# Three places in a RetNet and MLP kernel: where the down products fall back, in which banks a run begins, and when its last sums are formed

## The chip, the cores and the metric

The kernel runs on one core of a Trainium2 chip. A core has TensorE (PE in the profile), which multiplies matrices into PSUM; VectorE (DVE), ScalarE (ACT) and GpSimd (POOL) for elementwise work; and SyncE (SP), which here issues DMAs. Each engine follows its own stream of instructions in order, and the streams wait for each other through semaphores. The metric is the device time of one execution in microseconds, the median of several runs.

## The reference

```python
# q, k, v: (4, 8, 768, 64) float32; w_in: (512, 2048), w_out: (2048, 512)
for t in range(S):                      # RetNet recurrence, one decay gamma per head
    state = gamma * state + outer(k[:, :, t], v[:, :, t])
    y[:, :, t] = scale * q[:, :, t] @ state
x = y.transpose(0, 2, 1, 3).reshape(3072, 512)
h = x @ w_in
g = h - tanh(h)
out = g @ w_out                         # (3072, 512)
```

The kernel computes the recurrence in chunks of 128 tokens (24 chunks) and the MLP in blocks of 256 tokens (12 blocks, n = 0 to 11). The hidden dimension is cut into 8 pieces of 256 (m2 = 0 to 7). An "up" product gives h for one (n, m2), elementwise work ("shrink") gives g, and a "down" product adds g times a piece of w_out to the block's result.

## The kernel before

The MLP goes through steps, one (n, m2) each, counted from 0. Blocks 0 to 3 take the first 32 steps; from step 32 on, each block n = 4 to 11 is one run of 8 steps. From block 4 (FAST_UP) the up product, and from block 5 (FAST) the down product, is formed as a 2 by 2 block product with seven products in place of eight (Strassen's scheme in Winograd's form): fewer products for TensorE, more additions for the others.

```python
def fast_up(n, m2, some):               # products 1, 5, 7, 6 first, then 2, 3, 4
    if 1 in some:
        hps[n, m2] = bank("h", f"h_{n}_{m2}")       # two banks take turns
    ...
def up_take(n, m2):                     # the copy called fast_head in the profile
    nc.scalar.copy(out=odd_room[0], in_=hps[n, m2])
def up_pairs(): ...                     # GpSimd: sums of that copy
def up_add(n, m2): ...                  # VectorE: adds them into h, after products 2, 3, 4
```

Products 2, 3 and 4 of an up product write where 1, 5 and 7 were, so they wait for `up_take`.

A fast down product has seven products of 128x128 by 128x256. Product 1 and 2 share a bank ("first"), 5 and 7 another ("second"), 3 and 4 a third, and 6 has half of a bank of its own. Five banks rotate from run to run:

```python
def fast_banks(n):
    if not spare:
        t = banks("t", "fast_t")                         # one tile of two banks
        whole = y_banks.rearrange("p two r n t -> p r (two n t)")   # one tile of two banks
        o = [bank("o", "fast_o") for _ in range(2)]
        spare.append([t[:, 0], t[:, 1], o[0], whole[:, 0], whole[:, 1]])
        spare.append(o[1])
    five, sixth = spare
    first, second, third = five[:3]
    spare[0] = five[3:] + [first, second, third]
    acc = {1: first, 2: first, 5: second, 7: second, 3: third, 4: third, 6: sixth}
    ...
FAST_ORDER = (1, 2, 4, 6, 7, 5, 3)

def fast_end(n):                        # after the last tile of a run
    ...
    nc.scalar.copy(out=p1, in_=acc[1])
    add(c11, 2, p1)
    add(v_, 6, p1)
    for args in ((w_, 7, v_), (c22, 5, w_), (x_, 5, v_), (c21, 4, w_, True), (c12, 3, x_)):
        ending.append(lambda args=args: add(*args))      # one of these in each later step
```

`add` is a VectorE addition of a PSUM operand; after c21 and c12 it also issues the store of that half of the rows. The down product of a step lags behind the up product: `waiting` holds the tiles whose down product is due, and `downs(lag, half)` works off what is more than `lag` tiles back, in two halves (the first four and the last three products of a fast tile; the two row halves of a plain one). The main loop, cut to its order:

```python
for s in range(BEGUN, len(steps)):
    n, m2, first, last = steps[s]
    ci = with_chunk.get(s)              # a chunk in steps 9, 11, ... 45
    falls_back = s == FIRST_UP + 1      # FIRST_UP is 32
    lag = LAG + int(s >= FIRST_UP + 1)  # LAG is 2
    if ci is not None and not falls_back:
        chunk_step(ci)                  # chunk 17 in step 33, 21 in step 41
    ...
    fast_up(n, m2, (1, 5, 7, 6)); up_take(n, m2)
    if falls_back:
        chunk_step(ci)
    if before and ci is not None:
        turn_and_see(ci)                # begins the transposing DMA of chunk ci + 3
    waiting.append(steps[s])
    ... up_pairs(); GpSimd's further sums
    downs(lag, 0)
    fast_up(n, m2, (2, 3, 4)); up_add(n, m2); shrink_begin(n, m2)   # tanh, then square
    shrink_end(*before); fast_sums(*before)     # g of the step before; GpSimd's sums of g
    downs(lag, 1)
    end_some(1)                         # one waiting addition of the last run
    shrink_two(n, m2)
    ...                                 # middle(): ScalarE's next factor, q0
...
downs(0)
end_some(len(ending))
```

`chunk_step(ci)` holds the rest of chunk ci's products into y (outputs_rest), ScalarE's copies of y into x (keep_x), the products of chunk ci + 2 (which need its k and q transposed by DMA, kqT), the mask and the state on VectorE, and the first products of chunk ci + 1 into y.

Of the kernel before, what the change touches and what calls it, by code (L numbers as in the profile page):

```python
# [14 lines left out]
ALU = mybir.AluOpType  # L15
# [17 lines left out]
def kernel(  # L33
# [25 lines left out]
    nc = tc.nc  # L59
# [10 lines left out]
    NB = NCH // BLK  # L70
    BANK = 512
    TH = 2 * P
    LAG = 2
# [9 lines left out]
    op = ctx.enter_context(tc.tile_pool(name="op", bufs=4))  # L83
# [4 lines left out]
    def bank(tag, name):  # L88
        return ps.tile([P, BANK], F32, tag=tag, name=name)

    def banks(tag, name):

        return ps.tile([P, 2, BANK], F32, tag=tag, name=name, bufs=1)
# [112 lines left out]
    def convert(i):  # L206
        convert_begin(i)
        convert_bits(i)
        convert_end(i, nc.gpsimd)
# [201 lines left out]
    def work(tag, bufs):  # L411
        return tmp.tile([P, BANK], F32, tag=tag, name=tag, bufs=bufs)
# [95 lines left out]
    def rows_of(n):  # L508

        return out[ds(n * TH, TH)].rearrange("(p two) c -> p two c", two=2)  # L510
# [13 lines left out]
    steps = [(n, m2, i == 0, i == len(r) - 1) for r in runs for i, (n, m2) in enumerate(r)]  # L524
# [37 lines left out]
    def fast_weights(m2):  # L562

        b11, b12, b21, b22 = (w2[:, 2 * m2 + i, ts(c, TH)] for i in range(2) for c in range(2))
        t = {k: next(late_room) for k in (2, 3, 4)}
        t[1] = b12
        for k, x, y in ((3, b22, b12), (1, b12, b11), (2, b22, t[1]), (4, t[2], b21)):
            nc.gpsimd.tensor_tensor(t[k], x, y, op=ALU.subtract)
        t_of[m2] = t
# [18 lines left out]
    accs = {}  # L588

    def fast_banks(n):  # L590
        if not spare:
            t = banks("t", "fast_t")
            whole = y_banks.rearrange("p two r n t -> p r (two n t)")
            o = [bank("o", "fast_o") for _ in range(2)]
            spare.append([t[:, 0], t[:, 1], o[0], whole[:, 0], whole[:, 1]])
            spare.append(o[1])
        five, sixth = spare
        first, second, third = five[:3]
        spare[0] = five[3:] + [first, second, third]
        acc = {1: first, 2: first, 5: second, 7: second, 3: third, 4: third, 6: sixth}  # L600
        right = {2: 1, 7: 1, 4: 1, 6: n % 2}
        accs[n] = {k: b[:, ts(right.get(k, 0), TH)] for k, b in acc.items()}

    FAST_ORDER = (1, 2, 4, 6, 7, 5, 3)

    def fast_down(n, m2, first, last, some=FAST_ORDER):
        if first and 1 in some:
            fast_banks(n)
        left = fast_g[n, m2]
        for k in some:  # L610
            right = (
                w2[:, 2 * m2, :TH], w2[:, 2 * m2 + 1, :TH], w2[:, 2 * m2 + 1, TH:],
                *(t_of[m2][x] for x in (4, 1, 2, 3)),
            )[k - 1]

            nc.tensor.matmul(accs[n][k], left[k - 1], right, start=first and k in (1, 6, 7, 4),  # L616
                             stop=last, skip_group_check=True)

    ending = []

    def fast_end(n):


        acc = accs.pop(n)
        o = op.tile([P, 2, DM], F32, tag="sum", name=f"sum_{n}")
        c11, c12, c21, c22 = (o[:, j, ts(c, TH)] for j in range(2) for c in range(2))
        some = [mid.tile([P, 2, TH], F32, tag="a", name=f"fast_{n}") for _ in range(2)]
        p1, v_, x_, w_ = (t[:, i] for t in some for i in range(2))

        def add(dst, k, b, sub=False):  # L630
            if sub:
                nc.vector.tensor_tensor(dst, b, acc[k], op=ALU.subtract)
            else:
                nc.vector.tensor_tensor(dst, acc[k], b, op=ALU.add)
            if dst is c21 or dst is c12:
                j = int(dst is c21)
                nc.sync.dma_start(out=rows_of(n)[:, j], in_=o[:, j])

        nc.scalar.copy(out=p1, in_=acc[1])
        add(c11, 2, p1)  # L640
        add(v_, 6, p1)
        for args in ((w_, 7, v_), (c22, 5, w_), (x_, 5, v_), (c21, 4, w_, True), (c12, 3, x_)):
            ending.append(lambda args=args: add(*args))

    def end_some(n):
        for _ in range(min(n, len(ending))):
# [13 lines left out]
    def up_weights(m2):  # L660

        a11, a12, a21, a22 = (w1[:, ds(2 * c, 2), ts(2 * m2 + i, P)]
                              for i in range(2) for c in range(2))
        s_ = {k: next(up_room).rearrange("p (c m) -> p c m", c=2) for k in (2, 3, 4)}
        s_[1] = a21
        for k, x, y, how in ((3, a11, a21, ALU.subtract), (1, a21, a22, ALU.add),
                             (2, s_[1], a11, ALU.subtract), (4, a12, s_[2], ALU.subtract)):
            nc.gpsimd.tensor_tensor(s_[k], x, y, op=how)
        s_of[m2] = (a11, a12, s_[4], a22, s_[1], s_[2], s_[3])
# [22 lines left out]
    def up_take(n, m2):  # L692
        nc.scalar.copy(out=odd_room[0], in_=hps[n, m2])  # L693
# [15 lines left out]
    def part(j, n, m2, first, last):  # L709
        down(n, m2, j, first, last)  # L710
        if last:
            add_up(n, m2, j)

    def downs(lag, half=None):

        while len(waiting) > lag:
            tile_ = waiting[0] if half == 0 else waiting.pop(0)
            if tile_[0] >= FAST:
                some = (FAST_ORDER[:4], FAST_ORDER[4:], FAST_ORDER)[2 if half is None else half]
                fast_down(*tile_, some=some)  # L720
                if tile_[3] and half != 0:
                    fast_end(tile_[0])
            else:
                for j in range(2) if half is None else (half,):
                    part(j, *tile_)
            if half is not None:
                return
# [62 lines left out]

    FIRST_UP = steps.index((FAST_UP, 0, True, False))
    FIRST_DOWN = steps.index((FAST, 0, True, False))
    with_sums = {}
    for m2 in range(PAIRS):
        with_sums.setdefault(FIRST_UP - 4 + m2, []).append(lambda m2=m2: up_weights(m2))
        with_sums.setdefault(FIRST_DOWN + m2, []).append(lambda m2=m2: fast_weights(m2))

# [39 lines left out]
    def turn_and_see(ci):  # L837
        if ci + 3 < NCH:
            turn_by_dma(ci + 3)
        if FIRST <= ci + 1 < NCH - 1:  # L840
            if not before:
                outputs(ci + 1)
            see(ci + 1)

    for s in range(BEGUN, len(steps)):
        n, m2, first, last = steps[s]
        fast = n >= FAST_UP
        ci = with_chunk.get(s)

        falls_back = s == FIRST_UP + 1  # L850
        lag = LAG + int(s >= FIRST_UP + 1)
        if ci is not None and not falls_back:
            chunk_step(ci)
        for i in with_weights.get(s, []):
            convert(i)
            load_weights(i + 3)
        if fast:
            fast_up(n, m2, (1, 5, 7, 6))
            up_take(n, m2)
        else:  # L860
            for i in range(2):
                up(n, m2, i)
# [3 lines that stand above are left out]
            turn_and_see(ci)  # L866
        if ci == NCH - 2:
            outputs(ci + 1)
            see(ci + 1)
        waiting.append(steps[s])  # L870
        if fast:
            if before and ci is None:
                shrink_factors(*before)
                shrink_last_factor(*before)
            up_pairs()
            for make in with_sums.get(s, []):
                make()
            downs(lag, 0)
            fast_up(n, m2, (2, 3, 4))
            up_add(n, m2)  # L880
            shrink_begin(n, m2)
            if before:
                shrink_end(*before)
                if before[0] >= FAST:
                    fast_sums(*before)
            downs(lag, 1)
            end_some(1)
            shrink_two(n, m2)
            before = n, m2
            if s + 1 not in with_chunk:  # L890
                middle()
        else:
            shrink_begin(n, m2)
            shrink_factors(n, m2)
            shrink_multiply(n, m2)
            downs(lag)
            shrink_last_factor(n, m2)
            shrink_end(n, m2)
            for make in with_sums.get(s, []):
                make()  # L900
        if s + 1 in with_chunk:
            for which in range(2):
                scale(with_chunk[s + 1] + 3, which, nc.gpsimd)
# [60 lines left out]
```

## Time and profile before

| | us |
|---|---|
| median of 3 runs (lowest, highest) | 716.61 (716.52, 716.99) |
| span of the profiled execution | 716.1 |
| mean of one product of a fast down tile (two records each) | 0.38 a record |
| addition of 128x256 on VectorE (L634) | about 0.42 |
| the same on GpSimd (L568) | about 0.73 |
| store of a half of the rows, issue to landing | 2.0 to 2.3 |

The page gives for each engine the busy time, its share of the span and the number of instructions. A float32 product shows as two records of TensorE, and their ends are modelled, so records overlap: what a product costs is read from the distance between starts (1.73 us for four products of 128x256, from 700.82 to 702.55, for instance), not from the sum of durations. In a timeline, each row has the start and the duration in us, the engine, the line, the operation, the tile written and the tiles read, and in brackets the idle time of the engine before it with what ended it.

### The profile page before, as it was taken

The page shows a single profiled execution, that of the slowest core. Times are in us where ns is not written, and L with a number is a line of the kernel's source. Part 1 is how long each engine was busy: PE and PEld are TensorE (multiplying, and loading weights), DVE is VectorE, ACT ScalarE, POOL GpSimd, SP SyncE. Part 2 cuts the span into 40 slices and gives each one's busy share as a digit, 9 for nine tenths or more (in the row PEclk, how much of TensorE's full clock was granted, in tenths as well). Part 3 has the DMA queues.
Part 4 walks back from the last instruction along what each step waited for, and adds up shares of the span by engine and source line. Part 5 has one row for each costly group of instructions (what it writes and reads, how often), then busy time and mean ns, then how long its engine had stood idle before and what let it go on. Part 6 is the DMA issues. An engine that isn't in the chain of part 4 may idle for free.

```text
span 716.1 us, 16724 instructions
## 1 busy us (share of the span) xinstructions
PE 699.4 (98%) x6574; PEld 573.4 (80%) x6574; DVE 579.1 (81%) x977; ACT 431.9 (60%) x813; POOL 347.6 (49%) x492
## 2 busy tenths in 40 slices
PE   8899999999999999999999999999999999999996
PEld 8676666667667776766779989989999999999995
DVE  4999988898898856788777888788788787887885
ACT  4567566776777745565655555665555555666652
POOL 0564436454445572565277854453353544544432
PEclk9999999999999999999999999999999999999999
DMA  9873428866965565564200000000000000000000
GB/s 202 214 203 101 106 68 202 215 163 164 213 172 160 119 171 154 133 163 105 61 31 1 1 2 16 16 1 31 1 1 31 1 1 31 0 16 16 2 30 30
DMA packets 125406, 59.95 MB, mean 84 GB/s; under 512 B 109840, under 2 KB 118160, under 8 KB 125328
## 3 DMA queue, kind: packets, MB, share of 16 engines
q1 hardware_dynamic: 122880, 50.34, 29.2%
q10 hardware_dynamic: 2448, 8.54, 3.1%
q8 instruction: 52, 0.85, 0.5%
q14 instruction: 26, 0.21, 0.1%
HBM read 35.80 MB, written 14.68 MB: 70 GB/s over the span
## 4 chain that ended last, share of the span: by engine, by line
PE 85%; DVE 7%; ACT 3%; DMA 2%; POOL 1%; issue 1%; ACTq 0%; DVEq 0%; POOLq 0%
PE h L688 27%; PE o L490 16%; PE h L421 12%; PE fast_t L616 8%; PE y L616 8%; PE fast_o L616 7%; PE y L357 3%; DMA kqT<-rows 1%; PE s L309 1%; PE kqTp L217 1%; DVE head L190 1%; PE s L303 1%; DVE power L192 1%; DVE head L188 1%; PE kqTp L255 1%
## 5 line engine op out<-in xcount | busy, mean ns | idle before, releaser
L490 PE MATMUL o<-w,g 128*128 128x512 f32 x320 | 146.0, 594 | 0.0
L434 ACT ACTIVATE th<-h 128x512 f32<-128x512 f32 x64 | 38.2, 597 | 140.8 <-DVE h L705 138.3
L421 PE MATMUL h<-xT,w 128*128 128x256 f32 x512 | 117.7, 382 | 1.1 <-DVE w L204 1.1
L421 PEld LDWEIGHTS h<-xT,w 128*128 128x128 f32 x512 | 95.7, 190 | 20.9 <-issue 7.2
L578 POOL TENSOR_TENSOR s<-g 128x128 f32<-128x128 f32 x56 | 25.7, 459 | 167.0 <-DVE g L482 156.3
L490 PEld LDWEIGHTS o<-w,g 128*128 128x128 f32 x320 | 58.9, 190 | 54.4 <-issue 51.9
L688 PEld LDWEIGHTS h<-xT,w 128*128 128x128 f32 x512 | 76.2, 191 | 15.7 <-issue 7.1
L200 POOL TENSOR_TENSOR low<-low,power 128x512 f32<-128x512 f32 x30 | 38.7, 1288 | 101.7 <-DVE power L192 65.4
L482 DVE COPY_PREDICATED g<-large,th 128x512 f32<-128x512 int32 x96 | 77.0, 802 | 9.5
L688 PE MATMUL h<-xT,w 128*128 128x128 f32 x512 | 78.9, 277 | 1.0 <-ACT fast_head L693 0.9
L459 DVE TENSOR_TENSOR th<-h,th 128x512 f32<-128x512 f32 x96 | 65.5, 682 | 16.0 <-ACT th L432 14.7
L465 DVE SCALAR_TENSOR_TENSOR h<-q,h 128x512 f32<-128x512 f32 x96 | 66.9, 696 | 11.5 <-ACT q L440 1.5
L703 DVE TENSOR_TENSOR h<-h,fast_head 128x256 f32<-128x256 f32 x64 | 27.6, 432 | 56.8 <-PE h L688 56.1
L440 ACT ACTIVATE q<-u,tab 128x512 f32<-128x512 f32 x96 | 69.8, 727 | 1.7
L698 POOL TENSOR_TENSOR fast_head<-fast_head 128x256 f32<-128x256 f32 x64 | 47.4, 740 | 46.1 <-ACT fast_head L693 34.5
L448 ACT ACTIVATE q<-u,tab 128x512 f32<-128x512 f32 x96 | 69.5, 724 | 0.0
L449 ACT ACTIVATE large<-u,tab 128x512 f32<-128x512 f32 x96 | 68.5, 714 | 0.0
L688 PE MATMUL h<-x,w 128*128 128x128 f32 x448 | 68.3, 275 | 0.0
L460 DVE SCALAR_TENSOR_TENSOR h<-u,h 128x512 f32<-128x512 f32 x96 | 65.9, 686 | 0.0
L688 PEld LDWEIGHTS h<-x,w 128*128 128x128 f32 x448 | 59.0, 192 | 0.0
L693 ACT COPY fast_head<-h 128x512 f32<-128x512 f32 x64 | 37.5, 585 | 26.4 <-PE h L688 26.2
L474 DVE SCALAR_TENSOR_TENSOR g<-q,h 128x512 f32<-128x512 f32 x64 | 44.0, 687 | 7.8 <-ACT q L448 1.3
(190 smaller groups left out, 1465.8 us busy)
## 6 DMA issues: line engine op xcount, KB each, us to landing
rows<-apart ACTq DMA_DIRECT2D x16, 512.0 KB, 4.2
k<-in_k_dram SPq DMA_DIRECT2D x24, 256.0 KB, 4.5
q<-in_q_dram SPq DMA_DIRECT2D x24, 256.0 KB, 4.9
v<-in_v_dram SPq DMA_DIRECT2D x24, 256.0 KB, 5.4
raw<-in_moe_w_out_dram SPq DMA_DIRECT2D x12, 512.0 KB, 4.2
out_dram<-sum SPq DMA_DIRECT2D x24, 256.0 KB, 2.0
raw<-in_moe_w_in_dram SPq DMA_DIRECT2D x14, 256.0 KB, 4.4
raw<-in_moe_w_in_dram SPq DMA_DIRECT2D x28, 128.0 KB, 4.2
```

The costliest lines, as they stand in the source:

```text
L421: nc.tensor.matmul(hp, w1[:, c, ts(2 * m2 + i, P)], xT[n // 2][:, c, ts(n % 2, TH)], start=(i == 0 and c == 0), stop=(c == NC - 1), skip_g ...
L440: nc.scalar.activation(q0, shrinking[n, m2][0], AF.Square, bias=bias0)
L448: nc.scalar.activation(q1, u, AF.Square, bias=bias1, scale=math.sqrt(A))
L449: nc.scalar.activation(large, u, AF.Relu, bias=bias_m)
L459: nc.vector.tensor_tensor(th, hp, th, op=ALU.subtract)
L460: nc.vector.scalar_tensor_tensor(hp, in0=u, scalar=R, in1=hp, op0=ALU.subtract, op1=ALU.mult, reverse0=True)
L465: nc.vector.scalar_tensor_tensor(hp, in0=shrinking[n, m2][2], scalar=C0, in1=hp, op0=ALU.add, op1=ALU.mult)
L482: nc.vector.copy_predicated(flat, large.bitcast(I32), th)
L490: nc.tensor.matmul(o_p[j], gT[n, m2][:, i, ts(j, P)], w2[:, 2 * m2 + i], start=(first and i == 0), stop=(last and i == 1))
L616: nc.tensor.matmul(accs[n][k], left[k - 1], right, start=first and k in (1, 6, 7, 4), stop=last, skip_group_check=True)
L688: nc.tensor.matmul(hps[n, m2][:, ts(PLACE[k], P)], s_of[m2][k - 1][:, c], x_of[n][k - 1][:, c], start=(k == 1 and c == 0), stop=(c == 1), ...
L698: nc.gpsimd.tensor_tensor(odd_room[1], first[:, :2], first[:, 3:1:-1], op=ALU.add)
```

## The change

It has three parts.

- The lag grows from two tiles to three at step 41 (the 42nd step, the second of block 5) and not at step 33. The step in which it grows has no down products; there the chunk's work stands between the two parts of the up product. That was chunk 17 and is now chunk 21. The purpose is to keep the shorter distance while the down products are still plain ones, and to fall back where no further transposing DMA hangs on it.
- The first tile of a run takes its products in the order 1, 2, 7, 5 and then 4, 6, 3, so that it begins in the two banks that the run before did not use and comes to the third, which that run's sums are still read from, in its second half. The last run also swaps its second and third bank and begins with 1, 2, 4, 3.
- The last tile of all forms its sums between its products: the copy of product 1 and c11 after products 1 and 2, and so on. c22 moves to GpSimd, by way of a ScalarE copy of product 5, so that GpSimd reads it from SBUF. One half of the rows is stored from ScalarE's queue, the other from SyncE's.

The sums and products are the same as before; only their places, engines and order differ. The diff:

```diff
--- before.py
+++ after.py
@@ -595,17 +595,28 @@
             spare.append([t[:, 0], t[:, 1], o[0], whole[:, 0], whole[:, 1]])
             spare.append(o[1])
         five, sixth = spare
+        if n == 2 * NB - 1:
+
+            five[1:3] = five[2], five[1]
         first, second, third = five[:3]
         spare[0] = five[3:] + [first, second, third]
         acc = {1: first, 2: first, 5: second, 7: second, 3: third, 4: third, 6: sixth}
         right = {2: 1, 7: 1, 4: 1, 6: n % 2}
         accs[n] = {k: b[:, ts(right.get(k, 0), TH)] for k, b in acc.items()}
 
-    FAST_ORDER = (1, 2, 4, 6, 7, 5, 3)
-
-    def fast_down(n, m2, first, last, some=FAST_ORDER):
+
+    def fast_order(n, first):
+        if not first:
+            return (1, 2, 4, 6, 7, 5, 3)
+        return (1, 2, 4, 3, 7, 6, 5) if n == 2 * NB - 1 else (1, 2, 7, 5, 4, 6, 3)
+
+    def fast_down(n, m2, first, last, half=None):
+        some = fast_order(n, first)[{None: slice(7), 0: slice(4), 1: slice(4, 7)}[half]]
         if first and 1 in some:
             fast_banks(n)
+        fast_products(n, m2, first, last, some)
+
+    def fast_products(n, m2, first, last, some):
         left = fast_g[n, m2]
         for k in some:
             right = (
@@ -618,10 +629,9 @@
 
     ending = []
 
-    def fast_end(n):
-
-
-        acc = accs.pop(n)
+    def sums_of(n):
+
+        acc = accs[n]
         o = op.tile([P, 2, DM], F32, tag="sum", name=f"sum_{n}")
         c11, c12, c21, c22 = (o[:, j, ts(c, TH)] for j in range(2) for c in range(2))
         some = [mid.tile([P, 2, TH], F32, tag="a", name=f"fast_{n}") for _ in range(2)]
@@ -632,15 +642,52 @@
                 nc.vector.tensor_tensor(dst, b, acc[k], op=ALU.subtract)
             else:
                 nc.vector.tensor_tensor(dst, acc[k], b, op=ALU.add)
-            if dst is c21 or dst is c12:
-                j = int(dst is c21)
-                nc.sync.dma_start(out=rows_of(n)[:, j], in_=o[:, j])
-
-        nc.scalar.copy(out=p1, in_=acc[1])
-        add(c11, 2, p1)
-        add(v_, 6, p1)
-        for args in ((w_, 7, v_), (c22, 5, w_), (x_, 5, v_), (c21, 4, w_, True), (c12, 3, x_)):
-            ending.append(lambda args=args: add(*args))
+
+        def store(j, queue=nc.sync):
+            queue.dma_start(out=rows_of(n)[:, j], in_=o[:, j])
+
+        todo = {
+            "p1": lambda: nc.scalar.copy(out=p1, in_=acc[1]), "c11": lambda: add(c11, 2, p1),
+            "v": lambda: add(v_, 6, p1), "w": lambda: add(w_, 7, v_),
+            "c22": lambda: add(c22, 5, w_), "x": lambda: add(x_, 5, v_),
+            "c21": lambda: add(c21, 4, w_, True), "c12": lambda: add(c12, 3, x_),
+        }
+
+        def late_c22():
+            p5 = work("q0", 1)[:, :TH]
+            nc.scalar.copy(out=p5, in_=acc[5])
+            nc.gpsimd.tensor_tensor(c22, p5, w_, op=ALU.add)
+
+        return todo, store, late_c22
+
+    def fast_end(n):
+
+
+        todo, store, _ = sums_of(n)
+        for x in ("p1", "c11", "v"):
+            todo[x]()
+        for x in ("w", "c22", "x", "c21", "c12"):
+            def step(x=x):
+                todo[x]()
+                if x[:2] == "c1" or x == "c21":
+                    store(int(x == "c21"))
+            ending.append(step)
+
+    def finish(n, m2, first, last):
+
+        todo, store, late_c22 = None, None, None
+        for some, then in (((1, 2), ("p1", "c11")), ((6,), ("v",)), ((7, 5), ("w", "x")),
+                           ((4, 3), ("c21", "c12"))):
+            fast_products(n, m2, first, last, some)
+            if todo is None:
+                todo, store, late_c22 = sums_of(n)
+            for x in then:
+                todo[x]()
+                if x == "w":
+                    late_c22()
+                if x == "c21":
+                    store(1, nc.scalar)
+        store(0)
 
     def end_some(n):
         for _ in range(min(n, len(ending))):
@@ -716,8 +763,10 @@
         while len(waiting) > lag:
             tile_ = waiting[0] if half == 0 else waiting.pop(0)
             if tile_[0] >= FAST:
-                some = (FAST_ORDER[:4], FAST_ORDER[4:], FAST_ORDER)[2 if half is None else half]
-                fast_down(*tile_, some=some)
+                if tile_ == steps[-1]:
+                    finish(*tile_)
+                    return
+                fast_down(*tile_, half=half)
                 if tile_[3] and half != 0:
                     fast_end(tile_[0])
             else:
@@ -790,6 +839,7 @@
 
     FIRST_UP = steps.index((FAST_UP, 0, True, False))
     FIRST_DOWN = steps.index((FAST, 0, True, False))
+    FALL = FIRST_DOWN + 1
     with_sums = {}
     for m2 in range(PAIRS):
         with_sums.setdefault(FIRST_UP - 4 + m2, []).append(lambda m2=m2: up_weights(m2))
@@ -847,8 +897,8 @@
         fast = n >= FAST_UP
         ci = with_chunk.get(s)
 
-        falls_back = s == FIRST_UP + 1
-        lag = LAG + int(s >= FIRST_UP + 1)
+        falls_back = s == FALL
+        lag = LAG + int(s >= FALL)
         if ci is not None and not falls_back:
             chunk_step(ci)
         for i in with_weights.get(s, []):
```

## The prediction

> **What bounds the kernel now.** I read the page's table of busy time first, then the busy time by stretch, then TensorE's waits, and then the timeline of the three places that the change touches.
>
> ```profile
> PE 699.4 (98%) x6574; PEld 573.4 (80%) x6574; DVE 579.1 (81%) x977; ACT 431.9 (60%) x813; POOL 347.6 (49%) x492
> ```
>
> TensorE (PE) is busy 98% of the span, and the change removes no product. So all it can win is TensorE's idle time: 716.1 - 699.4 = 16.7 us at most. The stretches say where that lies (columns: length, then busy us of PE, PEld, DVE, ACT, POOL; clock; DMA share; GB/s):
>
> ```profile
> 288.00:327.00 39.00, 36.84 (x542) 27.43 (x541) 29.68 (x47) 23.10 (x47) 26.45 (x31) 1.00 0.53 136
> 327.00:372.00 45.00, 45.00 (x493) 32.48 (x494) 33.34 (x57) 27.33 (x58) 21.07 (x28) 1.00 0.26 71
> 424.00:704.00 280.00, 279.13 (x1895) 261.41 (x1894) 228.25 (x406) 165.26 (x279) 122.77 (x245) 1.00 0.03 12
> 704.00:717.00 13.00, 6.05 (x29) 4.97 (x27) 4.72 (x10) 0.37 (x1) 1.74 (x4) 0.87 0.11 40
> ```
>
> The reader is to see three pockets: 2.16 us idle where the seven-product up form begins (steps 32 to 37, counted from 0), 0.87 us in the long stretch of seven-product tiles, and the tail after the last product. From 327 to 372 it never stops. TensorE's waits name the causes:
>
> ```profile
> PE s L309 <- DMA kqT<-rows: 1.8, 2, 1.1
> PE h L688 <- ACT fast_head L693: 0.9, 1, 0.9
> PE fast_t L616 <- ACT q L448: 0.4, 1, 0.4
> PE y L616 <- ACT q L448: 0.4, 1, 0.4
> ```
>
> One of the two DMA waits (1.07 us, at 309.81) and the wait for fast_head (0.91 us, at 304.55) follow the step in which the down products fall back, which is step 33 now. The last two rows are the first tiles of runs 6 and 7. The ACT row they name has nothing to do with these banks, so I looked at the timeline there:
>
> ```profile
> 424.44 1.03 PE L616 MATMUL y<-w,g 128*128 128x256 f32 x4
> 425.34 0.42 DVE L634 TENSOR_TENSOR fast<-fast_t,fast 128x256 f32<-128x256 f32 x1
> 425.88 0.30 PEld L616 LDWEIGHTS fast_t<-fast_apart,g 128*128 128x128 f32 x2 [0.81 <-ACT fast_head L693]
> 425.91 0.67 PE L616 MATMUL fast_t<-fast_apart,g 128*128 128x256 f32 x2 [0.44 <-ACT q L448]
> ```
>
> Products 1 and 2 go into a bank of y. Product 4 then goes into a bank of fast_t and starts 0.15 us after VectorE's w addition, which reads the other bank of fast_t, has ended (425.76). So a wait here reaches over the two banks of one tile. The tail:
>
> ```profile
> 709.46 0.59 PE L616 MATMUL fast_t<-w,s 128*128 128x256 f32 x2
> 709.65 0.37 ACT L639 COPY fast<-y 128x256 f32<-128x256 f32 x1 [5.93 <-PE y L616]
> 710.06 0.42 DVE L634 TENSOR_TENSOR sum<-y,fast 128x256 f32<-128x256 f32 x1 [3.72 <-ACT fast L639]
> 712.31 0.41 DVE L634 TENSOR_TENSOR sum<-fast_t,fast 128x256 f32<-128x256 f32 x1
> 712.42 0.82 SPq L637 DMA_DIRECT2D out_dram<-sum  x2
> ```
>
> The copy of product 1, ready since about 707.5, starts at 709.65; seven additions follow in a row and end at 712.72. From there to the end at 716.1 there is only the store, 3.4 us.
>
> **What the Trainium skill says.** "Perfetto Trace Analysis", section Optimization Strategy: find the gaps of the most contended engine and what releases them. The rows above are those gaps. "PSUM — Partial Sum Buffer", section PSUM bank collisions raise a hardware error: any two of TensorE, ScalarE and VectorE on one bank and quadrant collide, reads with reads too, so such accesses are ordered. The trace agrees: VectorE's first shrink operation needs only tanh(h), yet it starts only when ScalarE has also finished its square of the same bank:
>
> ```profile
> 294.30 0.60 ACT L434 ACTIVATE th<-h 128x512 f32<-128x512 f32 x1 [3.86 <-DVE h L705]
> 294.80 0.59 ACT L435 ACTIVATE u<-h 128x512 f32<-128x512 f32 x1
> 295.42 0.69 DVE L459 TENSOR_TENSOR th<-h,th 128x512 f32<-128x512 f32 x1 [1.21 <-ACT u L435]
> ```
>
> "SBUF — State Buffer", section Who interferes with whom: a VectorE operation with both inputs in SBUF and a GpSimd operation block each other. The second addition of up_add has such inputs: 0.30 us in most steps, 0.60 us at 422.10 beside GpSimd's up_tokens. "DMA: Bandwidth & Descriptors", section Anatomy of one DMA (another issuing path): about 2 us of a DMA are fixed. The stores of sum take 2.0 to 2.3 us to land, so an earlier last store moves the end one for one.
>
> **The change, part by part.** In a step of seven-product up, TensorE needs 1.78 + 1.34 us for the up products and 1.72 + 1.72 us for the plain down products: 6.56 us, which the starts at 317.80 and 324.36 confirm. A step with a chunk takes 8.84 us (355.51 to 364.35).
>
> Part A, the fall-back moves from step 33 to step 41. The falling step has no down products, and its chunk stands between its up products. I compare the steps from 33 to 42. Now, from the timeline: step 33 takes 5.46 us (294.44 to 299.90), step 34 takes 7.81 us and step 35 takes 10.09 us (307.71 to 317.80). So the fall costs 7.81 - 6.56 = 1.25 us in step 34 (ScalarE comes late with its copy of h, after two copies for the transposing DMA of 1.05 us each) and 10.09 - 8.84 = 1.25 us in step 35 (TensorE has run ahead of that transposing DMA). After the change:
> - Step 33 is an ordinary chunk step. Like step 37 (9.19 us) it comes when GpSimd is full, and there y waits 0.35 us for ScalarE's keep_x. I take 9.19 us.
> - Step 34: 6.56 us. Step 35: the rows go out at about 301.55 and take 8.35 us to stand as kqT, as now (301.36 to 309.7), so at 309.9, and are wanted at about 310.8. No DMA wait; I take 9.0 us, with a little for keep_x.
> - Step 41 falls: 5.46 us as step 33 now. Its chunk is number 21. No transposing DMA is left to begin (chunk 24 does not exist), and one of the two state additions drops out.
> - Step 42: TensorE wants the copy of h at T + 9.04 (T is the start of step 41; 303.48 - 294.44). Now the second up_add ends at T + 7.37, and tanh, square, q0 and the copy stand in its way. Without the second state addition (0.34 us) it ends at about T + 7.03; with 0.1 to start tanh, 1.74 to the copy and 0.62 for it, T + 9.5. So some 0.5 us are lost: 7.06 us.
>
> Steps 36 to 40 do not change, given that g is ready one tile earlier. It is: in the present trace the g of two steps before is finished 0.65, 0.49 and 1.09 us before the down products of steps 36, 38 and 40 begin. The sums: now 5.46 + 7.81 + 10.09 + 8.84 + 6.56 = 38.76; after 9.19 + 6.56 + 9.0 + 5.46 + 7.06 = 37.27. **A wins 1.5 us** (0.6 to 2.0).
>
> Part B, the order of the first tile. Runs 6 and 7 lose 6.82 - 6.15 = 0.67 us each (420.19 to 427.01, and 470.05 to 476.87, against 6.15 in other steps). In the new order 1, 2, 7, 5 the products 7 and 5 go to the second bank. For run 6 that is the other bank of y, which run 5 never used; for run 7 it is a bank of fast_o, drained steps earlier. Product 4 comes some 2.2 us later, when w is long done. The other first tiles lose nothing now. **B wins 2 x 0.67 = 1.3 us.**
>
> Part C, the last tile. Its products take 7 x 0.43 us from 706.87 as before, and I write times on the present clock. Product 2 ends at 707.89, so p1 is copied at 707.93 (0.37), c11 at 708.34, v after product 6 at 708.76. Product 5 ends at 709.18: w from 709.22 to 709.64. Then ScalarE copies product 5 from the bank that w and x also read, so the three go one after the other: copy to 710.06, x to 710.52. GpSimd forms c22 beside it (0.74 us), done near 710.9. Product 3 ends at 710.05, so c21 (710.44) and c12 follow x at VectorE's pace and end at 711.19. The last store is issued near 711.25 in place of 712.82. GpSimd's s2 (707.48) and s3 (707.89) are ready before products 6 (707.73) and 7 (708.16). **C wins 1.6 us** (1.3 to 2.0).
>
> Together 1.5 + 1.3 + 1.6 = 4.4 us: 716.6 - 4.4 = 712.2 us.
>
> **The rivals.** First, the bubble of the fall merely moves: step 42 again loses 1.25 us and steps 33 or 35 wait for keep_x. For it: ScalarE's chain of tanh, square, q0 and copy stays. Against it: the DMA wait cannot return, since no transposing DMA follows. A falls to 0.6, time 713.1. Second, with one tile less of distance the down products wait for g. For it: only 0.49 us of room in step 38, and GpSimd is full in steps 33 to 35, so VectorE may be slowed there. It would cost 0.3 to 0.6 us: 712.6. Third, the tail becomes bound by GpSimd's c22 or by two stores at once from two queues: C falls to 1.2, time 712.6. Fourth, on the good side, ScalarE's copy and VectorE's reads of product 5's bank overlap and the fall costs nothing: 711.3.
>
> **Range and chances.** The parts hardly depend on each other. A carries most of the doubt, then C; B is a measured gap. Rivals one to three seldom meet, so I take 711.2 to 713.2. Faster by 2% would need 14.3 us, nearly all of TensorE's idle time, the start included; slower by 2% would need a stall in every step. Faster 0.005, within 2% 0.985, slower 0.01.
>
> **What would show it.** A: the wait of h L688 for fast_head near 304 and the DMA wait near 310 are gone, and one wait of about 0.5 us stands near step 42. B: the two waits of L616 at the first tiles of runs 6 and 7 are gone. C: from the last product to the last store some 1.4 us in place of 3.4. The prediction is wrong if down products of steps 33 to 40 wait for g, if step 42 waits longer than now step 34 does, or if the last store lands later than 2.3 us after its issue.

## The result, and the profile after

The changed kernel takes 712.25 us (median of 6 runs, 711.43 to 713.22) against 716.93 us of the kernel before beside it. The ratio is 0.9935, with a 95% interval of 0.9922 to 0.9947: 4.7 us less, 3.8 to 5.6. The change of 0.65% is under 2%, as predicted, and the time lies within the predicted range.

The page's busy times:

```profile
PE 699.3 (98%) x6574; PEld 574.5 (81%) x6574; DVE 576.8 (81%) x976; ACT 432.2 (61%) x814; POOL 348.5 (49%) x493
```

TensorE does the same work (699.3 against 699.4 us) in a span of 710.8 in place of 716.1 us. One addition has left VectorE; a copy on ScalarE and an addition on GpSimd have come. The busy times of the stretches, columns as before:

```profile
288.00:327.00 39.00, 38.77 (x514) 27.96 (x516) 29.12 (x47) 22.58 (x46) 26.66 (x31) 1.00 0.52 134
327.00:372.00 45.00, 44.82 (x592) 33.74 (x584) 35.15 (x61) 30.18 (x63) 21.89 (x31) 1.00 0.29 77
420.00:700.00 280.00, 280.00 (x1906) 262.90 (x1905) 229.49 (x408) 166.29 (x281) 123.42 (x247) 1.00 0.03 12
```

The first pocket has shrunk from 2.16 to 0.23 us of idle time. The second stretch, full before, now holds the fall-back and loses 0.18 us. In the long stretch of seven-product tiles nothing is left. Two of TensorE's waits:

```profile
PE s L309 <- DMA kqT<-rows: 1.1, 2, 0.6
PE h L735 <- ACT fast_head L740: 0.2, 1, 0.2
```

The waits of L627 (the fast down products, L616 before) for a bank are gone, and no down product waits for g. The DMA waits that remain lie ahead of step 32, in code that is the same. From step 32 on TensorE has two waits, of 0.2 us each: the one for fast_head and one of y for ScalarE's copies of y into x (keep_x). The first tile of run 6:

```profile
422.00 1.03 PE L627 MATMUL y<-w,g 128*128 128x256 f32 x4
422.87 0.59 PE L627 MATMUL y<-fast_v,s 128*128 128x256 f32 x2
422.89 0.42 DVE L644 TENSOR_TENSOR fast<-fast_t,fast 128x256 f32<-128x256 f32 x1
425.07 0.60 PE L627 MATMUL fast_t<-fast_apart,g 128*128 128x256 f32 x2
```

After products 1 and 2 comes 7 without a gap (0.87 us after product 1), and product 4 goes to fast_t 3.07 us after product 1. VectorE's w addition, which reads the other bank of fast_t, has then been done for 1.76 us (423.31). The tail:

```profile
705.66 0.59 PE L627 MATMUL y<-w,s 128*128 128x256 f32 x2
705.94 0.37 ACT L658 COPY q<-fast_t 128x256 f32<-128x256 f32 x1 [1.44 <-DVE fast L644]
706.35 0.42 DVE L644 TENSOR_TENSOR fast<-fast_t,fast 128x256 f32<-128x256 f32 x1 [0.49 <-ACT q L658]
706.39 0.72 POOL L659 TENSOR_TENSOR sum<-q,fast 128x256 f32<-128x256 f32 x1 [1.91 <-ACT q L658]
707.01 0.42 DVE L644 TENSOR_TENSOR sum<-y,fast 128x256 f32<-128x256 f32 x1
707.17 0.34 ACTq L647 DMA_DIRECT2D out_dram<-sum  x1
707.46 0.33 SPq L647 DMA_DIRECT2D out_dram<-sum  x1
```

The first row is product 3, the last of all; x is the addition at 706.35 and c12 the one at 707.01. When the last product runs, only ScalarE's copy, x, c21, c12 and GpSimd's c22 are still to begin. VectorE's x waits for ScalarE's copy of the same bank, as worked out.

### The profile page after: what moved, and what is told of

It reads as the page before. It is cut to its first block, busy times and chain, and to the rows that moved or that the text cites. A ratio compares the mean times of both kernels' runs of the same rounds, so it can differ in the third digit from the quotient of the medians.

```text
span 710.8 us, 16725 instructions
## 1 busy us (share of the span) xinstructions
PE 699.3 (98%) x6574; PEld 574.5 (81%) x6574; DVE 576.8 (81%) x976; ACT 432.2 (61%) x814; POOL 348.5 (49%) x493
## 4 chain that ended last, share of the span: by engine, by line
PE 89%; DVE 4%; DMA 2%; ACT 2%; POOL 1%; issue 1%; SPq 0%; DVEq 0%; ACTq 0%; POOLq 0%
PE h L735 28%; PE o L490 16%; PE h L421 13%; PE fast_t L627 9%; PE y L627 8%; PE fast_o L627 7%; PE y L357 3%; PE kqTp L217 1%; PE s L303 1%; PE s L309 1%; PE kqTp L255 1%; DMA kqT<-rows 1%; DMA raws<-in_moe_w_in_dram 1%; DVE head L190 1%; DVE head L188 1%
```

## How the traces are compared

Parts of one or two microseconds are near the spread of the times, so I read them as distances in the traces. In the traces of all kernels here, the start of step 32 lies between 286.5 and 288.7 us, although the code up to there is the same in all. The distances after it repeat to a few hundredths where the code is the same, but for steps 33 to 35 with the fall at step 33, where a DMA decides, as the part on why the prediction was right shows. A step is counted here from its first up product to the next step's first up product, so the chunk that opens a step counts to the step before it. The "first down step" of a run is the step in which its first tile's down product is formed (step 51 for run 6, 59 for run 7); a later step of the same kind takes 6.15 us.

| kernel | steps 32 to 42 | steps 43 to 45 | first down step of runs 6, 7 | first product of last tile to last store | last store to end |
|---|---|---|---|---|---|
| before | 83.5 | 20.52 | 6.83, 6.82 | 5.98 | 3.2 |
| changed | 81.5 | 20.19 | 6.15, 6.15 | 4.39 | 3.4 |
| fall only | 81.5 | 20.19 | 6.83, 6.79 | 5.98 | 3.2 |
| order only | 83.8 | 20.47 | 6.15, 6.15 | 6.42 | 3.2 |
| tail only | 83.1 | 20.51 | 6.83, 6.82 | 4.39 | 3.4 |

All in us. From the start of step 32 to the end of the span the kernel before takes 428.2 us and the changed one 423.1 us.

## The experiments

**The three parts alone.** In `e1_fall_only` the only edit of the kernel before is:

```diff
-        falls_back = s == FIRST_UP + 1
-        lag = LAG + int(s >= FIRST_UP + 1)
+        falls_back = s == FIRST_DOWN + 1
+        lag = LAG + int(s >= FIRST_DOWN + 1)
```

> Only the fall-back is moved from step 33 to step 41; the order of first tiles and the tail are as before. My theory: steps 33 to 42 take 36.8 us in place of 38.8 (a gain of 2.0), and the 0.33 us that TensorE loses in step 45 before (VectorE's up_add slowed beside a GpSimd operation) are gone as well, because the fall shifts GpSimd's work: 716.9 - 2.3 = 714.6 us. Rival: the 0.33 us of step 45 belong to the new order of the first tile, then the gain is 2.0 and step 45 still loses 0.33. Runs 6 and 7 still lose 0.67 us each in their first step.

Measured: ratio 0.9969 (0.9957 to 0.9980), 2.2 us less (1.4 to 3.1). Steps 32 to 42 take 2.0 us less and step 45 takes 6.25 in place of 6.58 us. So the gain of step 45 belongs to the fall, as my theory had it. The first down steps of runs 6 and 7 lose their 0.67 us as before.

`e2_order_only` is the changed kernel with the old fall and without the branch that leads to the new tail:

```diff
-    FALL = FIRST_DOWN + 1
+    FALL = FIRST_UP + 1
...
-                if tile_ == steps[-1]:
-                    finish(*tile_)
-                    return
```

> Only the order of the first tile of a run (and the last run's swapped banks); the fall stays at step 33, the tail forms its sums after the last product. My theory: the first steps of runs 6 and 7 take 6.15 in place of 6.82 us, a gain of 1.3 us and nothing else: 715.6 us. Rival as in the run before: step 45 gains 0.33 us too, then 715.3.

Measured: ratio 0.9986 (0.9978 to 0.9993), 1.0 us less (0.5 to 1.6). Both first steps lose nothing, as expected, and step 45 keeps most of its loss (6.53 us), so the rival fails. But the sum is smaller than 1.3, and the table shows why: the tail has grown by 0.44 us, from 5.98 to 6.42. The swap of the last run puts products 4 and 3 in the tile of products 1 and 2, and the old tail copies product 1 only after all seven have been issued:

```profile
708.91 0.60 PE L627 MATMUL y<-w,s 128*128 128x256 f32 x2
709.54 0.37 ACT L650 COPY fast<-y 128x256 f32<-128x256 f32 x1 [6.37 <-PE y L627]
```

The copy waits for the last product, in y. In the kernel before, it waited for the last but one (709.65, with the last product begun at 709.46). I had not foreseen this; with the old tail the swap costs 0.44 us.

`e3_tail_only` is the changed kernel with the old fall and the order 1, 2, 4, 6, 7, 5, 3 for every tile:

```diff
-    FALL = FIRST_DOWN + 1
+    FALL = FIRST_UP + 1
...
-        if not first:
-            return (1, 2, 4, 6, 7, 5, 3)
-        return (1, 2, 4, 3, 7, 6, 5) if n == 2 * NB - 1 else (1, 2, 7, 5, 4, 6, 3)
+        return (1, 2, 4, 6, 7, 5, 3)
```

> Only the interleaved tail (with the last run's swapped banks, but the old order of products in first tiles). My theory: from the start of the last tile's first product to the issue of the last store 4.4 us in place of 5.95, the end 1.5 to 1.6 us earlier: 715.4 us. Rival: the store bounds the end, so an earlier issue is partly lost to a longer landing: gain under 1 us.

Measured: ratio 0.9984 (0.9975 to 0.9993), 1.1 us less (0.5 to 1.8). In the trace the last store is issued 4.39 us after the tile's first product, 1.59 us earlier, and 0.15 us of that is given back after the issue (3.4 against 3.2 us to the end). So 1.44 us are left, and by the trace the rival (a gain under 1 us) fails, though a little does come back; the times, 0.5 to 1.8, would not decide it. The gains of the three runs add up to 2.2 + 1.0 + 1.1 = 4.3 us; with the 0.44 us that the swap costs in the second, that is 4.7, as for the whole change.

**Does a wait reach over both banks of a tile?** `e4_other_banks` is the kernel before with another order of the rotating banks:

```diff
-        spare.append([t[:, 0], t[:, 1], o[0], whole[:, 0], whole[:, 1]])
+        spare.append([t[:, 0], o[0], t[:, 1], whole[:, 0], whole[:, 1]])
```

> The kernel before, with the five rotating banks begun as t0, o0, t1, w0, w1 in place of t0, t1, o0, w0, w1 (t0 and t1 are the two banks of one tile, w0 and w1 those of the y tile). Theory 1 (a wait reaches over both banks of a tile): run 6 loses nothing in its first step, as the w addition then reads o0 and product 4 goes to t0; run 7 still loses 0.67 us; run 9 loses 1.2 to 1.5 us, because its product 1 goes to t1 while w of run 8 reads t0; run 10 loses 0.4 to 0.7 us, its product 1 goes to t0 while c11 of run 9 reads t1. Theory 2 (product 4 waits only for the reads of its own bank, p1 and c11): runs 6 and 7 lose 0.67 us as before and runs 9 and 10 nothing.

TensorE's waits at fast down products (one run, 718.29 us; columns: total us, times, longest us):

```profile
PE fast_t L616 <- DVE fast L634: 1.3, 1, 1.3
PE y L616 <- ACT q L448: 0.4, 1, 0.4
PE fast_t L616 <- DVE sum L634: 0.4, 1, 0.4
```

The first down steps of runs 6, 7, 9 and 10 take 6.15, 6.83, 7.69 and 6.81 us, that is losses of 0, 0.68, 1.54 and 0.66. Theory 1 holds in all four places; theory 2 only in run 7, where the two agree. The long wait is run 9's, for "fast", the w addition in the other bank of the tile; the row that names ACT is run 7's, with the same misleading name as before. None of these products writes a bank that is still being read. That holds for the kernel before too: c11, the last to read the bank that product 4 of run 6 writes, ended at 424.97, 0.94 us ahead of product 4. What product 4 waited for was w in the other bank.

`e8_no_swap` asks the same of the tail; it is the changed kernel without

```diff
-        if n == 2 * NB - 1:
-            five[1:3] = five[2], five[1]
```

> The changed kernel without the last run's swap of second and third bank: 7 and 5 then go to w1, in the same tile as w0 of products 1 and 2; 4 and 3 go to t0. If a wait reaches over both banks of a tile, product 7 of the last tile waits for c11, which reads w0: it starts 0.7 to 0.8 us late, and the last store comes 5.1 us after the last tile's first product in place of 4.39. If a wait holds for one bank only, nothing changes (4.39).

Its wait, and product 7 in the timeline:

```profile
PE y L624 <- DVE sum L641: 0.6, 1, 0.6
```

```profile
705.21 0.67 PE L624 MATMUL y<-fast_state,s 128*128 128x256 f32 x2 [0.58 <-DVE sum L641]
```

Product 7 waits for c11 (the first "sum") and starts 0.75 us late, and the last store comes 5.21 us after the first product, not 4.39. In the new tail the swap is worth 0.8 us.

**What does the fall cost, and where?** `e5_fall_39` and `e6_fall_43` are the changed kernel with `FALL = FIRST_DOWN - 1` and `FALL = FIRST_DOWN + 3`.

> The changed kernel with the fall at step 39 in place of 41. Step 39 is the last chunk step in which a transposing DMA is begun (chunk 23, wanted in step 41). My theory: the fall costs 1.25 us in the step after it through ScalarE's two copies for that DMA and 1.25 us in the next chunk step through the DMA itself. So step 40 takes about 7.8 us (6.56 without loss) and step 41 about 10.1 us (8.84 without loss): about 2.0 us more than the changed kernel. Rival: step 33 was a bad place because GpSimd was full there with the sums of the up weights (done by step 35); then step 39 is as good as 41, within 0.3 us.

Measured: ratio 0.9967 (0.9954 to 0.9981). Steps 38 to 42 take 37.1 us, 2.1 us more than the 35.0 us of the changed kernel. Both waits of the old fall are there again (the first row sums three waits; the longest, 1.2 us, is the one after the fall):

```profile
PE s L309 <- DMA kqT<-rows: 2.3, 3, 1.2
PE h L735 <- ACT fast_head L740: 0.9, 1, 0.9
```

So it was the transposing DMA and its copies that made the fall dear, and not GpSimd's work on the up weights. Step 45 takes 6.55 us here: 0.30 of its 0.33 us are lost again, though the fall differs by only one chunk.

> The changed kernel with the fall at step 43 in place of 41, so that the first fast down product is two tiles behind in step 42 and three from step 44. My theory (what is left of the fall is ScalarE's chain of tanh, square, q0 and copy against TensorE's lead): the chunk of step 43 has less work for TensorE (about 1.2 us in place of 2.2) but no mask and no state for VectorE, so step 44 loses 0.0 to 0.5 us and the whole is the changed kernel's time within 0.4 us. Rival: the fast down product of step 42 waits for GpSimd's sums of g, 0.5 to 1 us more.

Measured: ratio 0.9940 (0.9921 to 0.9960), which the times can't tell from the changed kernel. In the trace, steps 32 to 45 take 102.5 us against 101.7, 0.7 us more, so my 0.4 was too narrow. Step 44 loses 0.26 us (6.89 in place of 6.63), within what I expected. The fast down product of step 42 waits for no sums of g, as I thought. But a wait that I had not named appears:

```profile
PE y L357 <- ACT xT L402: 1.1, 2, 0.9
```

In step 43 the first products of chunk 23 wait 0.9 us for ScalarE's keep_x of chunk 22: with no products of a further chunk between them, TensorE is there too early. Of the two places, step 41 has more other work for TensorE.

**What is left of the fall.** In the changed kernel, TensorE comes to products 2, 3 and 4 of step 42 before the copy of h:

```profile
364.39 0.72 ACT L440 ACTIVATE q<-u,tab 128x512 f32<-128x512 f32 x1
365.02 0.56 ACT L740 COPY fast_head<-h 128x512 f32<-128x512 f32 x1
365.64 0.71 PE L735 MATMUL h<-xT,w 128*128 128x128 f32 x4 [0.18 <-ACT fast_head L740]
```

`e9_q0_after_copy` has the c22 of `e7_c22_vector` below and puts q0 behind that copy:

```diff
             up_take(n, m2)
+            if s == FALL + 1:
+                middle()
...
-            if s + 1 not in with_chunk:
+            if s + 1 not in with_chunk and not falls_back:
                 middle()
```

> The changed kernel with c22 on VectorE (as in the run before with that) and, in the one step after the fall, ScalarE's factor q0 of the step before put behind the copy of h instead of ahead of it. My theory: what is left of the fall (0.46 us in step 42) is ScalarE's chain of tanh, square, q0 and copy; without q0 (0.62 us) ahead of it the copy is there before TensorE wants it, and step 42 takes 0.35 to 0.46 us less. The last store comes 4.3 us after the last tile's first product. Together 0.5 us less than the changed kernel. Rival: VectorE's third factor, which needs q0, then comes late and the loss moves to step 43 or 44: no gain but the tail's 0.1.

Its timeline at the same place:

```profile
365.18 0.59 ACT L738 COPY fast_head<-h 128x512 f32<-128x512 f32 x1
365.65 0.74 ACT L440 ACTIVATE q<-u,tab 128x512 f32<-128x512 f32 x1
366.24 0.61 PE L733 MATMUL h<-xT,w 128*128 128x128 f32 x4
```

The wait is gone, step 42 takes 7.06 in place of 7.50 us, and steps 43 to 45 stay at 20.19: nothing moves on to them. `e11_changed_again` ran beside it.

> The changed kernel once more, beside the run before, so that the two are compared on one chip: 4.7 us less than the kernel before, and about 0.5 us more than the run with q0 moved. Steps 33 to 42 and the tail as in its first profile.

Measured: `e9_q0_after_copy` 712.39 us, ratio 0.9927 (0.9914 to 0.9939), and the changed kernel 712.48 us, 0.9926 (0.9913 to 0.9940). From step 32 to the end the trace of `e9_q0_after_copy` takes 422.5 us against 423.1 us. So 0.6 us are seen there, 0.44 of them in step 42 and the rest in the tail. The times can't show them: in these two traces step 32 began at 288.7 and 287.6.

**Where c22 is formed.** `e7_c22_vector` is the changed kernel with

```diff
-        ... ((7, 5), ("w", "x")), ...
+        ... ((7, 5), ("w", "c22", "x")), ...
-                if x == "w":
-                    late_c22()
```

> The changed kernel with c22 on VectorE, straight from PSUM between w and x, in place of ScalarE's copy and GpSimd's addition. My theory (the tail after the last product is VectorE's chain w, copy, x, c21, c12): w, c22, x, c21, c12 then follow at VectorE's pace and the last store is issued 4.3 us after the last tile's first product, in place of 4.39: the same time within 0.2 us. Rival: taking c22 off VectorE is what wins the tail, then the last store comes 0.3 to 0.4 us later.

Measured: 711.44 us, ratio 0.9918 (0.9900 to 0.9935), the interval overlapping that of the changed kernel. The last store comes 4.27 us after the first product (4.39 before). The move to GpSimd wins nothing; what wins is that the sums are formed between the products.

**The 0.33 us of step 45.** In the kernel before, VectorE's second addition of up_add in step 44 meets an operation of GpSimd:

```profile
384.21 0.72 POOL L568 TENSOR_TENSOR fast_kqT<-w 128x256 f32<-128x256 f32 x1
384.29 0.80 DVE L705 TENSOR_TENSOR h<-fast_head 128x128 f32<-128x128 f32 x1
```

`e10_weights_later` is the kernel before with

```diff
-        with_sums.setdefault(FIRST_DOWN + m2, []).append(lambda m2=m2: fast_weights(m2))
+        with_sums.setdefault(FIRST_DOWN + m2 + int(m2 >= 4), []).append(lambda m2=m2: fast_weights(m2))
```

> The kernel before, with GpSimd's sums of the down weights for pieces 4 to 7 made one step later (steps 45 to 48 in place of 44 to 47), so that none stands beside VectorE's up_add in step 44. My theory: the 0.33 us lost in step 45 come from that up_add (its second addition took 0.80 in place of 0.30 us, both inputs in SBUF, beside a GpSimd operation), which makes ScalarE's chain in step 45 late. So the addition of step 44 takes about 0.3 us and step 45 loses nothing (6.25 from up to up in place of 6.58). Rival: chunk 23's copies on ScalarE in step 45 are the cause; then it stays at 6.58.

The same addition then:

```profile
383.92 0.30 DVE L705 TENSOR_TENSOR h<-fast_head 128x128 f32<-128x128 f32 x1
```

Step 45 takes 6.25 us: the 0.33 us are gone, with the same chunk copies on ScalarE. The other traces agree. In the five where that addition takes 0.75 to 0.80 us (the kernel before, `e2_order_only`, `e3_tail_only`, `e4_other_banks`, `e5_fall_39`), step 45 takes 6.53 to 6.58; in all with 0.30 to 0.47 it takes 6.25, but for `e6_fall_43`, whose fall lies just before. The slowing itself is not gone: in `e10_weights_later` and in the changed kernel the addition of step 45 takes 0.84 and 0.86 us, and there step 46 loses nothing (6.15).

The first down step of run 6 took 7.05 us in this run, 0.22 more than before, and here the row of the wait names w:

```profile
PE fast_t L616 <- DVE fast L634: 0.7, 1, 0.7
```

A VectorE operation ahead of the sums, copy_predicated, took 1.10 us in place of 0.75, so w ended 1.54 us after product 1 in place of 1.32, and product 4 again began 0.15 us after w. The whole took 717.52 us in one run.

## Why the prediction was right, and where its steps were not

The time came out at the middle of the range, partly by luck. The gain was 4.7 us and not 4.4, and the kernel before took 716.93 us beside it and not 716.61; the two errors, 0.3 us each, cancel in the level.

- **Part A was under-sized.** Predicted 1.5 us, and the trace has 2.0 in steps 32 to 42 and 0.33 in step 45. Counted as the prediction counts it (the chunk belongs to the step that it opens), the terms compare so: step 33 9.19, measured 8.83; step 35 9.0, measured 8.84; step 41 5.46, measured 5.53; step 42 7.06, measured 7.02. Step 33 failed most. I had added 0.35 us for y's wait on keep_x. It is there, but about 0.24 us long (y starts 0.70 us after s, against 0.46 in the kernel before at 356.83). And chunk 18 is the first of its sequence, so half of its products with the state don't exist (16 records in place of 32). For step 42, `e9_q0_after_copy` shows that the chain named for it is the cause. That step 45 would gain was missed: I looked for losses in the steps whose order changes, not in those where GpSimd's work only shifts in time.
- **The loss of the old fall is not a constant.** In the five traces with the fall at step 33, steps 32 to 42 take 83.1 to 83.8 us, as the transposing DMA comes sooner or later (TensorE waits 0.7 us there with the tail only, 1.4 with the order only). Part A is thus worth 1.6 to 2.3 us there. The five traces with the fall at step 41 and nothing else changed in these steps all give 81.5.
- **TensorE's lead is not all of that loss.** The working took it as given that the rows need 8.35 us to stand as kqT. In the changed kernel they need 6.78. The difference is mainly in the first of the two transfers, the rows: 4.13 us before, 2.63 after. With the fall at step 33 they go out 2.94 us after the last load of the chunk's k, q and v was issued (298.42, 301.36), while the DMA share, the page's busy share of the DMA engines, is 1.25 (301 to 302 us); in the changed kernel 4.61 us after it, at a share of 0.07. With 2.63 us for the rows, kqT would by estimate have stood at 308.3, ahead of TensorE's demand at 308.7. So the wait of 1.07 us needed the slow transfer as well as TensorE's lead. That the loads slow it is not tested; with the fall at step 39, where no loads are left, it is the transposing transfer that takes longer (5.85 us, 4.40 in the changed kernel), and the cause stays open.
- **Part B was right:** 0.67 us in each of runs 6 and 7, nothing elsewhere, and for the reason given (`e4_other_banks`).
- **Part C was right in its size and its chain,** 1.59 us to the issue against 1.6; copy, x and the last store came within 0.05 us of the working, counted from product 1. That "an earlier last store moves the end one for one" was nearly so: 0.15 us came back, as the second store landed 2.43 us after its issue, against 2.29 before. Landing later than 2.3 us was named as a sign of being wrong; it came true, at this small cost. "From the last product to the last store some 1.4 us in place of 3.4" does not fit the working, which has 1.8 from the start of the last product (709.46 to 711.25); measured, it is 1.80 in place of 3.38. That c22 goes to GpSimd, which the working took as given, is not what wins it (`e7_c22_vector`).
- **The sum.** The parts in the traces make 2.3 + 1.35 + 1.4 = 5.1 us, as does 428.2 - 423.1. The times show 4.7 us, and 5.1 is inside their interval (3.8 to 5.6). What the times lack is not assigned; the start of step 32 varies by more than that.

Of the rivals, the second (down products waiting for g) and the third (the tail bound by c22) did not occur. The first (a bubble that moves) occurred in the small: 0.46 us in step 42, as estimated. The fourth, the good one, did not: x waited for the copy, and the fall still costs those 0.46 us.

## What to carry to other kernels

Where one engine is busy 98% of the time, list its gaps in the timeline, name the operation that ends each, and price a change as the sum of the gaps that it closes and opens. A lag in a software pipeline can cost a bubble where it grows (0.5 us at step 41, about 2.5 at steps 33 and 39 here); grow it where that step has other work for the busy engine and where no transfer hangs on its lead. A wait can belong to a whole tile and not to the bank that is written, so rotate accumulators with that in mind. Allocating their banks as tiles of their own should do as well; no run here tried it.

## What was not expected of the hardware

VectorE's addition of two SBUF operands ended 0.16 us after the GpSimd operation that had begun 0.08 us before it, and took 0.80 in place of 0.30 us. That agrees with the Trainium skill, "SBUF — State Buffer", section Who interferes with whom, by which one of the two blocks the other. It holds throughout these traces: each of the 148 such additions of up_add that took over 0.35 us, in all 13 of them, ended 0.15 to 0.16 us after a GpSimd operation that had begun before it, so it waited that operation out. What was new to me is its reach: half a microsecond on VectorE, off TensorE's path, came out as 0.33 us on TensorE a step later.
